# Attention, a dense layer and an expert layer in one kernel: gate logits of three tiles on VectorE, and a first slot filled from twelve tiles

## The chip, the core and the metric

The program runs on one core of one Trainium2 chip. The metric is the device time of one execution in microseconds, as the median of several executions. A profiled execution has a time of its own, and the span of its trace is a little shorter than that time.

## What is computed

Three layers follow one another. All arithmetic is in float32; most matrix products are made as three passes over a high and a low part of each operand, so that they keep float32 accuracy.

```python
# attention: B=4, H=8, S=576, D=64, with rotary positions
attn_out = softmax(rot(q) @ rot(k).T / sqrt(D)) @ v
x = attn_out.transpose(0, 2, 1, 3).reshape(2304, 512)
# dense layer, w_in 512x2048, w_out 2048x512
h = maximum(x @ w_in, 0);  x = (h * h) @ w_out
# expert layer: 8 experts of 512x1024x512, one expert for each token
logits = x @ w_gate + modality_bias[modality_id]
e_idx = argmax(logits, 1);  gate_w = softmax(logits)[arange(N), e_idx]
for e in range(8):
    mask = e_idx == e
    out[mask] = gate_w[mask, None] * (maximum(x[mask] @ w1[e], 0) @ w2[e])
```

## The kernel before, in words

**Blocks and units.** The 2,304 tokens are 18 tiles of 128. The dense layer takes them in five blocks: four of 512 tokens and a fifth of 256 (`BLOCKS`). A block has 16 units, one for each 128 of the 2,048 hidden values; so there are 80 units, and units 64 to 79 are the fifth block. From unit 80 on a unit is one 128-wide chunk of an expert's hidden layer for one slot of tokens.

**One unit.** The loop at line 1092 writes the program in a fixed order. In unit q it writes what hangs in `pre[q]`, then the first half of unit q + 2 (`LA = 2`), then `mid[q]`, then the second half of unit q, then `post[q]`. Each engine works through its own instructions in that order. The first half (`first`, line 680) is: `mm1`, twelve matmuls into `h` (L659); `relu` on ACT (L665), `r` = max(h, 0) scaled; `square` on ACT (L669), which rounds r² into `gh`, the high part; `square_v` on DVE (L673), which puts r² unrounded into `h`; `rest` on DVE (L677), which makes the low part `gl` = h − gh. The second half (`mm2`, L695) adds gh and gl times the output weights into one PSUM bank for each tile.

**Banks.** `h` and all other short-lived PSUM tiles (`junk`, `tp`, `lp`, `rp`, `cp`, `mp`) share a ring of four banks (tag "b", `bufs=4`). In program order the fifth tile takes the bank of the first, and the engine that writes it waits until the last reader of the old one is done.

**Gate logits.** After a block's last unit its output tiles lie in SBUF as `ysb`. For blocks one to three the logits of their tiles are made on DVE by `lg_dve` (L707): one product of a tile with one expert's gate column, summed along the row, 32 for each block, three in a unit; each writes a `junk` bank. The gate columns, copied to all partitions, are the four `wgb` tiles of the tag "wraw". For block four (tiles 12 to 15, in units 64 to 68) and for tiles 16 and 17 they are made on TensorE: `lg_tr` turns a tile with four transposes (L713) and splits it (L716 on ACT, L717 on DVE) into `yt`; `lg_mm` makes eight matmuls into `lp` (L725), from which DVE takes the logits (L727, L728). `choose` then finds each token's expert and `ranks` its rank among the tokens of that expert (L756 to L758).

**Slots.** Experts work on slots of 256 tokens. The first slot (`NE = 2`, so 512 tokens) is filled early, from the most frequent expert among the first `NT0 = 16` tiles: `counts` and `early1` at the end of unit 69 find the expert and each token's position, `early2` (unit 71) turns that into a table with 16 matmuls (L787), `early3` (unit 72) makes indices of it, and four indirect DMAs (`gather`, L942, on POOL's queue) fetch 128 tokens each. `gtrans` (units 74 to 77) turns each gathered tile with four transposes (L952) and splits it in two halves: ACT makes the high part (L965), DVE the low part (L966) of each.

**Expert weights.** `eissue` (L926, on SP's queue) loads a 128-wide chunk of an expert's weights, 512 KB, into a "wraw" tile; `esplit` splits it on ACT (L932) and DVE (L933). The first four are issued from unit 71 on and split at the heads of units 73 to 76, the next four at the heads of units 80 to 83. The first expert half (`emm1`, L979) belongs to unit 80 and is written in unit 78.

**The rest of the table.** After tiles 16 and 17 (units 80 and 81) `final0` to `final4` give every other token a position, and a token of the early expert whose position is below `ET` = 512 stays in the first slot. A last branch (line 1110) runs further slots if more than nine are needed.

Of the kernel before, what the change touches and what calls it, by code (L numbers as in the profile page):

```python
# [9 lines left out]
F32 = mybir.dt.float32  # L10
F32R = mybir.dt.float32r
# [4 lines left out]
ACTF = mybir.ActivationFunctionType  # L16
ALU = mybir.AluOpType
# [434 lines left out]
WF = 2048 + 64  # L452
NE = 2
ET = NE * SLOT
SLOTS = NE + (NTOK - SLOT) // SLOT + E - 1
LAST = NTOK // SLOT - 1
NCOL = 2 * SLOTS
NT0 = 16
BIG = 65536.0
PASSES = ((0, 0), (0, 1), (1, 0))  # L460

# [55 lines left out]
def experts(tc, wts, ps, xT, rD, wexp, mod, wg, mb, cst, ident, yD, out):  # L517
    nc = tc.nc
    with ExitStack() as ctx:
# [10 lines left out]
        def small(shape, dt, name, tag=None):  # L530
            return sb.tile(shape, dt, name=name, tag=tag or name)
# [89 lines left out]
        off = small([128, 1], F32, "off")  # L621
        es0 = small([128, 1], I32, "es0")
        full = small([128, E], I32, "full")
        so, d = small([128, E], F32, "so"), small([128, 1], F32, "d_off")
        es, esi = small([1, SLOTS], F32, "es"), small([1, SLOTS], I32, "esi")
        nh, nhi, tn = small([1, 1], F32, "nh"), small([1, 1], I32, "nhi"), small([1, 1], F32, "tn")
        gv = small([128, NCOL], F32, "gv")
# [42 lines left out]

        def square_v(n):
            h = hs[n]
            nc.vector.scalar_tensor_tensor(out=h, in0=h, scalar=W_SC, in1=rs[n], op0=ALU.mult, op1=ALU.mult)  # L673

        def rest(n):
# [34 lines left out]
        def lg_tr(j):  # L710
            tp = bank([128, DM], "tp")
            for k in range(4):
                nc.tensor.transpose(tp[:, k * 128:(k + 1) * 128], ysb[j][:, k * 128:(k + 1) * 128], ident)  # L713
            t = wts.pool.tile([128, 2, DM], F32R, name="yt", tag="wraw", bufs=NRAW)
            hi, lo = t[:, 0], t[:, 1]
            nc.scalar.activation(out=hi, in_=tp, func=ACTF.Copy)  # L716
            nc.vector.tensor_tensor(out=lo, in0=tp, in1=f32(hi), op=ALU.subtract)  # L717
            yts[j] = hi, lo
# [41 lines left out]
        def counts(j):  # L760
            cp = bank([128, E], "cp")
            nc.tensor.matmul(out=cp, lhsT=one_b, rhs=cum[:, j], start=True, stop=True)
            tables["n"] = cp
# [32 lines left out]
        def early1():  # L796
# [15 lines left out]
            nc.vector.tensor_reduce(out=v_, in_=u, axis=AX.X, op=ALU.add)  # L812
            nc.vector.tensor_scalar(out=v_, in0=v_, scalar1=BIG, scalar2=None, op0=ALU.add)
            rc = split_pos(v_, NT0, "0")
            rhs = small([128, NT0, 2 * NE], F32R, "e_rhs", "et")
            shp = [128, NT0, 2 * NE]
            nc.vector.tensor_tensor(out=rhs, in0=c_io8[:, 0:2 * NE].unsqueeze(1).to_broadcast(shp),
# [12 lines left out]
        def final0():  # L830
            nc.vector.tensor_copy(out=val[:, :, 0], in_=c_id)
            nc.vector.tensor_copy(out=val[:, :, 1], in_=gate)
            nc.vector.tensor_tensor(out=val[:, :, 2], in0=gate, in1=f32(val[:, :, 1]), op=ALU.subtract)
            nc.vector.tensor_scalar(out=so, in0=ohs, scalar1=off, scalar2=None, op0=ALU.mult)
            nc.vector.tensor_scalar(out=d, in0=off, scalar1=-float(ET), scalar2=None, op0=ALU.add)

        def final1():
            cp = tables.pop("n")
# [25 lines left out]
            nc.vector.tensor_copy(out=esi, in_=es)  # L864
            nc.vector.scalar_tensor_tensor(out=add, in0=bc[:, 0], scalar=float(SLOT), in1=so,
                                           op0=ALU.mult, op1=ALU.subtract)
            v_, m_ = small([128, NT], F32, "f_v", "v_"), small([128, NT], F32, "f_m")
            nc.vector.tensor_tensor(out=tmp3, in0=add.unsqueeze(1).to_broadcast([128, NT, E]), in1=rank, op=ALU.add)
            nc.vector.tensor_tensor(out=tmp3, in0=tmp3, in1=oh, op=ALU.mult)
            nc.vector.tensor_reduce(out=v_, in_=tmp3, axis=AX.X, op=ALU.add)  # L870
            nc.vector.tensor_scalar(out=m_, in0=v_, scalar1=float(ET), scalar2=d, op0=ALU.is_lt, op1=ALU.mult)
            nc.vector.tensor_tensor(out=v_, in0=v_, in1=m_, op=ALU.add)
            tables["rc1"] = split_pos(v_, NT, "1")

        def final2():
# [141 lines left out]
        def at(d, n, *fs):  # L1017
            d.setdefault(n, []).extend(fs)

        at(mid, NFC - 1, load_wgb)  # L1020
        for b in range(NB):
# [9 lines left out]
            if b < 3:  # L1031
                jobs = [(j, e) for j in range(j0, j0 + nt) for e in range(E)]
                for q, (j, e) in enumerate(jobs):
                    at(mid, n0 + q // 3, lambda j=j, e=e: lg_dve(j, e))
                at(mid, n0 + 11, lambda j0=j0, nt=nt: choose(j0, j0 + nt))
                at(mid, n0 + 13, lambda j0=j0, nt=nt: ranks(j0, j0 + nt))
            elif b == 3:
                for t in range(4):
                    at(mid, n0 + t, lambda j=j0 + t: lg_tr(j))
                    at(mid, n0 + t + 1, lambda j=j0 + t: lg_mm(j))  # L1040
                at(mid, n0 + 4, lambda j0=j0: choose(j0, j0 + 4))
                at(post, n0 + 5, lambda j0=j0: ranks(j0, j0 + 4), lambda: counts(NT0), early1)
                at(post, n0 + 7, early2)
                at(mid, n0 + 7, lambda: [eissue(m) for m in range(M0, M0 + 3)])
                at(pre, n0 + 8, early3, lambda: [gather(c, True) for c in range(2 * NE)])
                for i in range(4):
                    at(pre, n0 + 9 + i, lambda m=M0 + i: esplit(m, m + 3))
                    at(mid, n0 + 10 + i, lambda t=i: gtrans(NE - 1, t))

        k0 = N - M0  # L1050
        at(mid, N, lambda: lg_tr(16), lambda: lg_tr(17))
# [7 lines left out]
           lambda: esplit(M0 + 10, M0 + 13),  # L1059
           lambda: [gather(2 * NE + 2 + t, False) for t in range(2)], lambda: second(M0 + 7))  # L1060
        for i in range(4):
            at(pre, N + i, lambda m=M0 + 4 + i: esplit(m, m + 3 if m + 3 < M0 + 8 else None))
        for m in range(M0 + 8, M1):
            u = {8: 4, 9: 5, 10: 6, 11: 7}.get(m - M0, m - 4 - M0) + N
            if u != N + 6:
# [169 lines left out]
```

## Time and profile before

| what | us |
|---|---|
| median of 3 runs | 920.58 (919.7 to 921.89) |
| the profiled execution | 921.56 |
| span of its trace | 919.8 |
| PE busy | 895.2 |
| DVE busy | 629.0 |
| ACT busy | 484.3 |

PE is TensorE's matmuls, PEld its weight loads, which run beside the matmuls; DVE is VectorE, ACT ScalarE, POOL GpSimd, SP the queue that issues most DMAs. A matmul's length in the trace contains its way through a pipeline, so lengths of single matmuls overlap; how far the work has moved is read from the starts. Around the span lie 1.76 us of the profiled execution's time. It is 0.98 us above the median.

### The profile page before, as it was taken

How to read it: one execution, taken by the hardware profiler on the slowest of the kernel's cores; microseconds unless marked ns; L12 is line 12 of the kernel's file. 1: busy time of each engine (PE TensorE's matmuls, PEld its weight loads, DVE VectorE, ACT ScalarE, POOL GpSimd, SP SyncE). 2: the span in 40 equal slices, each digit the busy share in tenths (PEclk: the TensorE clock that was granted, in tenths of full speed). 3: DMA queues.
4: the chain of work that ended last, by engine and by line, in shares of the span. 5: the costliest groups of instructions: out<-in, count | busy, mean ns of one | idle time of the engine just before them, and what ended most of it. 6: DMA issues, size and time to landing. Idle time of an engine off the chain costs nothing. (4 is left out here: it accounts for less than half of the span.)

```text
span 919.8 us, 14598 instructions
## 1 busy us (share of the span) xinstructions
PE 895.2 (97%) x5251; PEld 751.5 (82%) x5251; DVE 629.0 (68%) x1197; ACT 484.3 (53%) x956; POOL 287.1 (31%) x229
## 2 busy tenths in 40 slices
PE   7999999999999999999999999999999999999995
PEld 6778778778787887888888888888988899999994
DVE  7998898889888788466545545653655776666650
ACT  6888898868866674322332232224253265555541
POOL 2667687867535555010011001000020322112111
PEclk9999999999999999999999999999999999999998
DMA  5666646546446454410030003001241568767621
GB/s 174 195 167 200 186 150 180 177 110 186 143 146 211 135 183 117 133 35 1 1 116 23 0 1 92 1 1 46 68 140 46 176 205 262 230 220 241 203 93 36
DMA packets 46976, 115.65 MB, mean 126 GB/s; under 512 B 10272, under 2 KB 14384, under 8 KB 46896
## 3 DMA queue, kind: packets, MB, share of 16 engines
q1 hardware_dynamic: 43856, 104.94, 37.1%
q0 software_dynamic: 3040, 9.70, 2.9%
q8 instruction: 43, 0.70, 0.3%
q14 instruction: 37, 0.30, 0.1%
HBM read 92.56 MB, written 15.54 MB: 118 GB/s over the span
## 5 line engine op out<-in xcount | busy, mean ns | idle before, releaser
L665 ACT ACTIVATE r<-h 128x512 f32<-128x512 f32 (+1 forms) x80 | 44.1, 553 | 215.5 <-PE h L659 190.7
L659 PE MATMUL h<-xs,w 128*128 128x512 f32 (+1 forms) x660 | 143.8, 367 | 0.3 <-DVE gl L677 0.3
L673 DVE SCALAR_TENSOR_TENSOR h<-h,r 128x512 f32<-128x512 f32 (+1 forms) x80 | 51.4, 644 | 125.5 <-ACT r L665 125.3
L659 PEld LDWEIGHTS h<-xs,w 128*128 128x128 f32 x660 | 115.8, 188 | 22.0 <-DVE gl L677 0.8
L285 ACT ACTIVATE e<-sc,nmx 128x576 f32<-128x576 f32 x144 | 106.4, 740 | 35.3 <-DVE nmx L274 34.3
L695 PE MATMUL y<-w,gh 128*128 128x512 f32 x396 | 123.2, 392 | 1.2 <-POOL w L514 1.2
L274 DVE TENSOR_REDUCE nmx<-sc 128x1 f32<-128x576 f32 x144 | 106.2, 752 | 23.4 <-PE sc L269 20.1
L269 PE MATMUL sc<-kh,q 128*128 128x288 f32 (+1 forms) x336 | 95.9, 322 | 10.5 <-ACT e L285 9.4
L933 DVE TENSOR_TENSOR w<-eraw,w 128x1024 fp32r<-128x1024 f32 x64 | 78.4, 1225 | 33.9 <-ACT w L932 33.9
L269 PE MATMUL sc<-kl,q 128*128 128x288 f32 (+2 forms) x336 | 88.0, 298 | 0.0
L695 PEld LDWEIGHTS y<-w,gh 128*128 128x128 f32 x396 | 73.3, 188 | 16.4 <-POOL w L514 1.6
L269 PEld LDWEIGHTS sc<-kh,q 128*128 128x128 f32 x336 | 60.7, 189 | 29.0 <-ACT e L285 20.6
L327 PE MATMUL b<-ident,e 128*128 128x128 f32 x640 | 82.5, 275 | 1.1 <-ACT e L285 1.1
L577 POOL TENSOR_TENSOR xraw<-xraw,rbs 128x512 f32<-128x512 f32 (+1 forms) x14 | 16.0, 1148 | 197.5 <-DMA rbs<-rD 194.7
L695 PE MATMUL y<-w,gl 128*128 128x512 f32 x198 | 77.2, 390 | 0.2 <-DVE gl L677 0.2
L979 PEld LDWEIGHTS h<-ye,w 128*128 128x128 f32 x576 | 74.0, 189 | 3.7
L327 PEld LDWEIGHTS b<-ident,e 128*128 128x128 f32 x640 | 74.0, 142 | 1.7 <-ACT e L285 1.3
L979 PE MATMUL h<-ye,w 128*128 128x256 f32 x576 | 74.8, 280 | 0.0
L1002 PE MATMUL y<-w,ge 128*128 128x512 f32 x288 | 74.6, 394 | 0.0
L356 PE MATMUL b<-et,v 128*64 128x288 f32 x512 | 69.5, 412 | 0.0
L932 ACT ACTIVATE w<-eraw 128x1024 fp32r<-128x1024 f32 x64 | 67.4, 1052 | 4.0 <-DMA eraw<-wexp 4.0
L1009 POOL DMA_INDIRECT out<-ob,six x19 | 22.4, 1179 | 137.5 <-ACT ob L1008 105.3
(228 smaller groups left out, 1716.0 us busy)
## 6 DMA issues: line engine op xcount, KB each, us to landing
eraw<-wexp SPq DMA_DIRECT2D x64, 512.0 KB, 4.3
wraw<-wio SPq DMA_DIRECT2D x32, 512.0 KB, 5.2
rawq<-qx SPq DMA_DIRECT2D x15, 576.0 KB, 4.3
rawk<-kx SPq DMA_DIRECT2D x15, 576.0 KB, 4.0
v<-v SPq DMA_DIRECT2D x16, 320.0 KB, 4.8
yD<-ysb SPq DMA_DIRECT2D x18, 256.0 KB, 2.2
xT<-xo SPq DMA_DIRECT2D x12, 288.0 KB, 3.4
xraw<-xT SPq DMA_DIRECT2D x12, 256.0 KB, 2.9
```

The lines of the kernel that those rows point to most:

```text
L269: nc.tensor.matmul(out=o[:, x:x + w], lhsT=q[:, hd, q0:q0 + 128], rhs=k[:, hd, y:y + w], start=(n == 0), stop=(n == len(ops) - 1))
L274: nc.vector.tensor_reduce(out=m, in_=sc(p, j)[:, :, 0:HS], axis=AX.XY, op=ALU.max, negate=True)
L285: nc.scalar.activation(out=e(p)[:, o:o + S].rearrange("p (a b) -> p a b", a=2), in_=sc(p, j)[:, :, 0:HS], func=ACTF.Exp, bias=live[p, f"nm ...
L327: nc.tensor.transpose(t[:, i * 128:(i + 1) * 128], x[:, o:o + 128], ident)
L356: nc.tensor.matmul(out=o[64 * hd:64 * hd + 64], lhsT=lhsT, rhs=rhs, start=(c == 0), stop=(c == 4))
L659: nc.tensor.matmul(out=h, lhsT=w[:, a, k * 128:(k + 1) * 128], rhs=xs[b, k][:, c], start=(k == 0 and i == 0), stop=(k == 3 and i == 2))
L673: nc.vector.scalar_tensor_tensor(out=h, in0=h, scalar=W_SC, in1=rs[n], op0=ALU.mult, op1=ALU.mult)
L695: nc.tensor.matmul(out=yp[t], lhsT=g[a][:, t * 128:(t + 1) * 128], rhs=w[:, c, 512:1024], start=(begin and i == 0), stop=(f == NFC - 1 and ...
L932: nc.scalar.activation(out=w[:, 0], in_=r, func=ACTF.Copy)
L933: nc.vector.tensor_tensor(out=w[:, 1], in0=r, in1=f32(w[:, 0]), op=ALU.subtract)
L979: nc.tensor.matmul(out=h, lhsT=w[:, a, k * 128:(k + 1) * 128], rhs=x[:, c], start=(k == 0 and i == 0), stop=(k == 3 and i == 2))
L1002: nc.tensor.matmul(out=yp[s, t], lhsT=g[a][:, t * 128:(t + 1) * 128], rhs=w[:, c, 512:1024], start=(f == 0 and i == 0), stop=(f == EFC - 1 ...
```

## The change

- **Tiles 12 to 14.** Their logits are made in units 64 to 75 by `lg_dve`, 24 products, two in a unit. Tile 15 stays on TensorE. `choose` and `ranks` for tiles 12 to 15 move to units 78 and 79.
- **Squares.** In the fifth block `square_v` is a second Square on ACT instead of a product on DVE.
- **First slot.** `NT0` is 12. Its table is made at the end of units 61 and 63, and its indices at the head of unit 64; the gathers stay at the head of unit 72. `early1` writes the positions it gives into `pos0` and takes those tokens out of `oh`; `final1` adds `pos0` instead of comparing with `ET`. The formula for `SLOTS` gives 18 instead of 17, so `NCOL` is 36 instead of 34.
- **Buffers.** The `yt` tile moves from the tag "wraw" to "xs". The gate columns stay in "wraw" during the fifth block; a chunk of expert weights is issued (units 67, 70, 73 and 76) as each of their four tiles has had its last product. The first four chunks are split at the heads of units 76, 77, 79 and 80, and each issues the chunk four later.

```diff
--- before.py
+++ after.py
@@ -452,10 +452,10 @@
 WF = 2048 + 64
 NE = 2
 ET = NE * SLOT
-SLOTS = NE + (NTOK - SLOT) // SLOT + E - 1
+NT0 = 12
+SLOTS = NE + (NTOK - NT0 * 128 // E - E) // SLOT + E
 LAST = NTOK // SLOT - 1
 NCOL = 2 * SLOTS
-NT0 = 16
 BIG = 65536.0
 PASSES = ((0, 0), (0, 1), (1, 0))
 
@@ -621,7 +621,7 @@
         off = small([128, 1], F32, "off")
         es0 = small([128, 1], I32, "es0")
         full = small([128, E], I32, "full")
-        so, d = small([128, E], F32, "so"), small([128, 1], F32, "d_off")
+        so, pos0 = small([128, E], F32, "so"), small([128, NT0], F32, "pos0")
         es, esi = small([1, SLOTS], F32, "es"), small([1, SLOTS], I32, "esi")
         nh, nhi, tn = small([1, 1], F32, "nh"), small([1, 1], I32, "nhi"), small([1, 1], F32, "tn")
         gv = small([128, NCOL], F32, "gv")
@@ -670,6 +670,9 @@
 
         def square_v(n):
             h = hs[n]
+            if n >= NFC * (NB - 1):
+                nc.scalar.activation(out=h, in_=rs[n], func=ACTF.Square)
+                return
             nc.vector.scalar_tensor_tensor(out=h, in0=h, scalar=W_SC, in1=rs[n], op0=ALU.mult, op1=ALU.mult)
 
         def rest(n):
@@ -711,7 +714,7 @@
             tp = bank([128, DM], "tp")
             for k in range(4):
                 nc.tensor.transpose(tp[:, k * 128:(k + 1) * 128], ysb[j][:, k * 128:(k + 1) * 128], ident)
-            t = wts.pool.tile([128, 2, DM], F32R, name="yt", tag="wraw", bufs=NRAW)
+            t = sb.tile([128, 2, DM], F32R, name="yt", tag="xs", bufs=5)
             hi, lo = t[:, 0], t[:, 1]
             nc.scalar.activation(out=hi, in_=tp, func=ACTF.Copy)
             nc.vector.tensor_tensor(out=lo, in0=tp, in1=f32(hi), op=ALU.subtract)
@@ -812,6 +815,10 @@
             nc.vector.tensor_reduce(out=v_, in_=u, axis=AX.X, op=ALU.add)
             nc.vector.tensor_scalar(out=v_, in0=v_, scalar1=BIG, scalar2=None, op0=ALU.add)
             rc = split_pos(v_, NT0, "0")
+            nc.vector.scalar_tensor_tensor(out=pos0, in0=v_, scalar=off, in1=v_, op0=ALU.is_lt, op1=ALU.mult)
+            nc.vector.tensor_scalar(out=v_, in0=v_, scalar1=off, scalar2=None, op0=ALU.is_ge)
+            nc.vector.tensor_tensor(out=oh[:, 0:NT0], in0=oh[:, 0:NT0],
+                                    in1=v_.unsqueeze(2).to_broadcast([128, NT0, E]), op=ALU.mult)
             rhs = small([128, NT0, 2 * NE], F32R, "e_rhs", "et")
             shp = [128, NT0, 2 * NE]
             nc.vector.tensor_tensor(out=rhs, in0=c_io8[:, 0:2 * NE].unsqueeze(1).to_broadcast(shp),
@@ -832,7 +839,6 @@
             nc.vector.tensor_copy(out=val[:, :, 1], in_=gate)
             nc.vector.tensor_tensor(out=val[:, :, 2], in0=gate, in1=f32(val[:, :, 1]), op=ALU.subtract)
             nc.vector.tensor_scalar(out=so, in0=ohs, scalar1=off, scalar2=None, op0=ALU.mult)
-            nc.vector.tensor_scalar(out=d, in0=off, scalar1=-float(ET), scalar2=None, op0=ALU.add)
 
         def final1():
             cp = tables.pop("n")
@@ -864,12 +870,11 @@
             nc.vector.tensor_copy(out=esi, in_=es)
             nc.vector.scalar_tensor_tensor(out=add, in0=bc[:, 0], scalar=float(SLOT), in1=so,
                                            op0=ALU.mult, op1=ALU.subtract)
-            v_, m_ = small([128, NT], F32, "f_v", "v_"), small([128, NT], F32, "f_m")
+            v_ = small([128, NT], F32, "f_v", "v_")
             nc.vector.tensor_tensor(out=tmp3, in0=add.unsqueeze(1).to_broadcast([128, NT, E]), in1=rank, op=ALU.add)
             nc.vector.tensor_tensor(out=tmp3, in0=tmp3, in1=oh, op=ALU.mult)
             nc.vector.tensor_reduce(out=v_, in_=tmp3, axis=AX.X, op=ALU.add)
-            nc.vector.tensor_scalar(out=m_, in0=v_, scalar1=float(ET), scalar2=d, op0=ALU.is_lt, op1=ALU.mult)
-            nc.vector.tensor_tensor(out=v_, in0=v_, in1=m_, op=ALU.add)
+            nc.vector.tensor_tensor(out=v_[:, 0:NT0], in0=v_[:, 0:NT0], in1=pos0, op=ALU.add)
             tables["rc1"] = split_pos(v_, NT, "1")
 
         def final2():
@@ -1033,19 +1038,24 @@
                 for q, (j, e) in enumerate(jobs):
                     at(mid, n0 + q // 3, lambda j=j, e=e: lg_dve(j, e))
                 at(mid, n0 + 11, lambda j0=j0, nt=nt: choose(j0, j0 + nt))
-                at(mid, n0 + 13, lambda j0=j0, nt=nt: ranks(j0, j0 + nt))
+                if b < 2:
+                    at(mid, n0 + 13, lambda j0=j0, nt=nt: ranks(j0, j0 + nt))
+                    continue
+                at(post, n0 + 13, lambda j0=j0, nt=nt: ranks(j0, j0 + nt), lambda: counts(NT0), early1)
+                at(post, n0 + 15, early2)
+                at(pre, n0 + 16, early3)
             elif b == 3:
-                for t in range(4):
-                    at(mid, n0 + t, lambda j=j0 + t: lg_tr(j))
-                    at(mid, n0 + t + 1, lambda j=j0 + t: lg_mm(j))
-                at(mid, n0 + 4, lambda j0=j0: choose(j0, j0 + 4))
-                at(post, n0 + 5, lambda j0=j0: ranks(j0, j0 + 4), lambda: counts(NT0), early1)
-                at(post, n0 + 7, early2)
-                at(mid, n0 + 7, lambda: [eissue(m) for m in range(M0, M0 + 3)])
-                at(pre, n0 + 8, early3, lambda: [gather(c, True) for c in range(2 * NE)])
+                at(mid, n0, lambda j=j0 + 3: lg_tr(j))
+                at(mid, n0 + 1, lambda j=j0 + 3: lg_mm(j))
+                for q in range(3 * E):
+                    at(mid, n0 + q // 2, lambda j=j0 + q % 3, e=q // 3: lg_dve(j, e))
+                at(pre, n0 + 8, lambda: [gather(c, True) for c in range(2 * NE)])
                 for i in range(4):
-                    at(pre, n0 + 9 + i, lambda m=M0 + i: esplit(m, m + 3))
+                    at(mid, n0 + (3, 6, 9, 12)[i], lambda m=M0 + i: eissue(m))
+                    at(pre, n0 + (12, 13, 15, 16)[i], lambda m=M0 + i: esplit(m, m + 4))
                     at(mid, n0 + 10 + i, lambda t=i: gtrans(NE - 1, t))
+                at(mid, n0 + 14, lambda j0=j0: choose(j0, j0 + 4))
+                at(mid, n0 + 15, lambda j0=j0: ranks(j0, j0 + 4))
 
         k0 = N - M0
         at(mid, N, lambda: lg_tr(16), lambda: lg_tr(17))
@@ -1059,7 +1069,7 @@
            lambda: esplit(M0 + 10, M0 + 13),
            lambda: [gather(2 * NE + 2 + t, False) for t in range(2)], lambda: second(M0 + 7))
         for i in range(4):
-            at(pre, N + i, lambda m=M0 + 4 + i: esplit(m, m + 3 if m + 3 < M0 + 8 else None))
+            at(pre, N + i, lambda m=M0 + 4 + i: esplit(m))
         for m in range(M0 + 8, M1):
             u = {8: 4, 9: 5, 10: 6, 11: 7}.get(m - M0, m - 4 - M0) + N
             if u != N + 6:
```

## Rows read from the trace of the kernel before

**Rows 1.** Page: granted clock in 40 slices; expert weight issues (KB, us to landing)
```profile
PEclk9999999999999999999999999999999999999998
...
eraw<-wexp SPq DMA_DIRECT2D x64, 512.0 KB, 4.3
```

**Rows 2.** Windows: busy us (count) of PE, PEld, DVE, ACT, POOL; clock; DMA
```profile
628.00:684.00 56.00, 56.00 (x384) 51.37 (x383) 33.21 (x98) 23.51 (x53) 5.17 (x4) 1.00 0.31 104
684.00:737.00 53.00, 52.68 (x255) 43.19 (x255) 31.53 (x89) 15.36 (x24) 7.44 (x7) 1.00 0.29 100
```

**Rows 3.** Waits of PEld from 370 to 905 us: total, times, longest
```profile
PEld h L659 <- DVE gl L677: 0.8, 1, 0.8
PEld mp L787 <- DVE ohr L778: 0.7, 1, 0.7
```

**Rows 4.** Timeline, weight loads, unit with a transposed tile: start, length, engine
```profile
643.58 1.56 PEld L659 LDWEIGHTS h<-xs,we 128*128 128x128 f32 x12
...
645.99 0.42 PEld L713 LDWEIGHTS tp<-ident,ysb 128*128 128x128 f32 x4
...
647.65 1.60 PEld L659 LDWEIGHTS h<-xs,w 128*128 128x128 f32 x12
```

**Rows 5.** Timeline, a fifth-block unit without extra work
```profile
668.46 1.60 PEld L659 LDWEIGHTS h<-xs,w 128*128 128x128 f32 x12
...
669.98 0.30 PEld L695 LDWEIGHTS y<-w,gh 128*128 128x128 f32 x2
...
670.29 0.38 ACT L665 ACTIVATE r<-h 128x256 f32<-128x256 f32 x1 [1.01 <-PE h L659]
...
670.71 0.42 ACT L669 ACTIVATE gh<-r 128x256 fp32r<-128x256 f32 x1
670.71 0.43 DVE L673 SCALAR_TENSOR_TENSOR h<-h,r 128x256 f32<-128x256 f32 x1 [0.17 <-ACT r L665]
...
671.03 1.05 ACT L932 ACTIVATE w<-eraw 128x1024 fp32r<-128x1024 f32 x1
...
671.23 1.59 PEld L659 LDWEIGHTS h<-xs,w 128*128 128x128 f32 x12
```

**Rows 6.** Timeline, weight loads of the first slot's table, and the next unit's
```profile
663.88 1.98 PEld L787 LDWEIGHTS mp<-e_rhs,ohr 128*128 128x128 f32 x16
...
665.78 1.48 PEld L659 LDWEIGHTS h<-xs,w 128*128 128x128 f32 x12
```

**Rows 7.** Timeline, gate products on DVE in the fourth block
```profile
611.32 0.69 DVE L707 SCALAR_TENSOR_TENSOR junk<-ysb,wgb 128x512 f32<-128x512 f32 x1
...
611.92 0.73 DVE L707 SCALAR_TENSOR_TENSOR junk<-ysb,wgb 128x512 f32<-128x512 f32 x1
612.57 0.14 DVE L707 DVE_READ_ACCUMULATOR junk<-ysb,wgb 128x1 f32 x1
```

**Rows 8.** All gate products: duration ns min/median/max, first and last start
```profile
L707 DVE SCALAR_TENSOR_TENSOR junk<-ysb,wgb x96: 687/731/1226, 381.6 to 611.9; 128x512 f32<-128x512 f32 x96
```

**Rows 9.** Timeline, one gathered tile turned and split in two halves
```profile
677.91 0.42 DVE L677 TENSOR_TENSOR gl<-h,gh 128x256 fp32r<-128x256 f32 x1
678.25 0.41 DVE L966 TENSOR_TENSOR yee<-tp,yee 128x256 fp32r<-128x256 f32 x1
678.70 0.39 ACT L965 ACTIVATE yee<-tp 128x256 fp32r<-128x256 f32 x1 [1.33 <-DVE yee L966]
...
679.12 0.42 DVE L966 TENSOR_TENSOR yee<-tp,yee 128x256 fp32r<-128x256 f32 x1 [0.45 <-ACT yee L965]
```

**Rows 10.** Timeline, one tile of expert weights split
```profile
675.12 1.05 ACT L932 ACTIVATE w<-eraw 128x1024 fp32r<-128x1024 f32 x1
...
676.21 1.23 DVE L933 TENSOR_TENSOR w<-eraw,w 128x1024 fp32r<-128x1024 f32 x1 [0.52 <-ACT w L932]
```

**Rows 11.** Timeline, weight loads of the first expert unit
```profile
684.06 0.19 PEld L979 LDWEIGHTS h<-yee,w 128*128 128x128 f32 x1
...
684.68 2.38 PEld L979 LDWEIGHTS h<-yee,w 128*128 128x128 f32 x11 [0.43 <-DVE yee L966]
```

## Prediction, made before the changed kernel was run

> **What bounds the kernel now.** I read the windows of the stretch first, then the waits, then the timeline of single units. In the windows, look at the first two figures: from 628 to 684 us, the fifth block, PE is busy all the time, and from 684 to 737 us for 52.68 of 53 us [rows 2]. DVE has 33.21 and ACT 23.51 us of the 56. The waits say the same: between 370 and 905 us the longest of PE's weight loads are one of 0.8 us for `rest` and one of 0.7 us for the last table's one-hot rows [rows 3]. The clock is at its upper level (2.4 GHz), nine tenths of it or more, in every slice [rows 1]. So PE sets the end here, what leaves PE's program comes off the time, and every new wait of PE goes back on.
>
> The Trainium skill ("Trainium Kernel Development and Optimization", Performance Expectations) says that matmul busy time is a bad metric and weight-load busy share a good one. By it PE is at 51.37 of 56 us, 92% [rows 2], and its other 4.6 us would be room. The short list of waits [rows 3] speaks against it; it is rival four.
>
> **What leaves PE.** A unit with a transposed tile and a tile's logits lasts from weight load 643.58 to 647.65, 4.07 us [rows 4]. A unit with neither lasts from 668.46 to 671.23, 2.77 us [rows 5]. A tile so costs 1.30 us of PE, and three cost 3.90. The first slot's table takes 665.78 − 663.88 = 1.90 us for 16 matmuls [rows 6]; four fewer are 0.48. The last table keeps its 18 matmuls, six columns wider. Its price is bounded by nothing and by the width's share, 6% of the 1.90 us of a table of 16, 0.1 us; I take nothing: even matmuls of four columns took 0.12 us each in the first table [rows 6], so the weight loads set the pace. Together 4.38 us leave.
>
> **What comes to DVE and ACT, and why it doesn't pay in full.** Two products follow each other by 0.60 to 0.65 us [rows 7]; 24 are 15.6 us. DVE had 22.8 us free of the 56 [rows 2] and loses 16 squares of 0.43 us [rows 5], 6.9 us. ACT had 32.5 us free and gains 16 squares. No row shows a Square into PSUM; the nearest is L669, the same shape from the same tile into SBUF, at 0.42 us [rows 5]. I take 0.42, with 0.38 (the relu out of PSUM, same size) and 0.6 as bounds. So both have room in sum. What counts is when a bank of the ring comes free, because the junk tiles turn in it too. I time one unit from its first weight load, using rows 5: relu starts at 1.83, the first square at 2.25, the next ACT instruction at 2.57 (the weight split's place at 671.03). That is now the second square; it ends at 2.99, and DVE starts `rest` 0.04 later, as it does after relu, at 3.03. `rest` takes 0.42 and lets the next DVE instruction start after 0.34 [rows 9], so h is free at 3.45, the products start at 3.37 and 4.02, and the second one's bank is free at 4.02 + 0.65 + 0.14 = 4.81.
>
> - *Units 66 to 73.* In program order each unit takes h, junk, junk. The h of two units later takes the second junk's bank at 2 × 2.77 = 5.54. It is free 0.73 us before. No wait, though each unit hangs on this margin.
> - *Unit 64.* One transposed tile adds a bank, so the next h takes the bank of the h before. PE is there at 2.77 + 0.42 [rows 4] = 3.19, and the bank is free at 3.45. A weight load goes ahead of a waiting matmul (one stood at 684.06 before the pause) [rows 11], which takes some 0.1 us off: 0.15 us; bounds nothing and 0.3.
> - *Unit 74, first gathered tile.* It takes the bank of unit 73's second product, free at 4.81 − 2.77 = 2.04 of unit 74; PE is there when h is through, at 1.52 (669.98 − 668.46) [rows 5]. Wait: 0.5 us.
> - *Unit 75, second gathered tile.* It takes the bank of the first. DVE does `rest` and two products before that tile's low parts, which start at 4.67. The halves go by turns: ACT's second half starts 0.45 after DVE's first, DVE's second 0.42 after that [rows 9]: 5.12 and 5.54, and the bank is free at 5.96. PE passed the first tile at 2.04 + 0.42, began the next h after the second half's 1.25 (671.23 − 669.98) [rows 5] at 3.71 and is there at 5.23. Wait: 0.7 us.
> - *Unit 78, first expert unit.* It waits for the fourth gathered tile's first half: 0.62 us from 684.06 to 684.68, of which the row gives 0.43 as idle [rows 11]. Before it, ACT now has a weight split of 1.05 us [rows 10] at the heads of units 76 and 77, two squares more, and the second tile's half that came late. Carrying the same steps on from 5.96, the fourth tile's first low part ends at about 15.6 where PE is there at 14.0: 1.6 us instead of 0.62, so 0.9 more. Bounds: nothing more, if ACT catches up, and the 1.05 of one whole split on top, 2.0.
>
> These are 2.25 us. The sum: −4.38 + 2.25 = −2.1 us.
>
> At the gathered tiles the trace shows ACT idle for 1.33 us until DVE's half is done, although the halves are different columns [rows 9]. The Trainium skill ("PSUM — Partial Sum Buffer", PSUM bank collisions raise a hardware error) says that accesses of two engines have to be kept apart by bank and not by address; the row agrees. Without that order the second tile would wait some 0.2 us instead of 0.7 and the sum would be −2.6; by the rule and the row it is −2.1.
>
> **What I cost at nothing.** The making of the first table moves to units 61 to 63, with three more small DVE steps and one group of one-hot rows fewer. Those units take 512 columns, so DVE's burst has longer units for cover than before, where it caused none of the long waits [rows 3]; with the cover gone the table's matmuls would wait, as the last table's do, 0.7 us. The eight weight loads only change places. SP has no other transfer between unit 64 and the last two tiles' stores; a load lands in 4.3 us [rows 1], and the tightest, issued in unit 76 and split at the head of unit 80, has four units, over 11 us. It stands behind a load that waits for the first split's low part, one split's 1.23 us [rows 10]; without this cover PE would wait for `esplit`. The gathers keep their place in POOL's queue, and their table is ready eight units earlier. `choose` and `ranks` cost PE three short matmuls in either place; in unit 79 they stand behind the first `gel`, bounds nothing and 0.5 us. In the last table's chain DVE loses two small steps and gets 6% wider products; its wait of 0.7 us [rows 3] stays. `yt` in "xs" frees ACT and DVE in units 80 to 82, where PE did not wait for them: nothing. Routing: the first 12 tiles must hold 512 tokens of their commonest expert, or a tenth slot would run the last branch. With seed 0 I counted 772 of them in the reference's routing, 764 of the next, and both versions come to the same ten slots with the last half not used: no branch.
>
> **Rivals.**
> 1. *No bank waits.* If PE's loads run ahead further than I allow and ACT's square ends earlier, units 64 and 74 to 78 wait as little as before. All 4.4 us come off: 916.2. For it: PE waited for a bank once in the whole stretch [rows 3]. Against: there no unit had two products and a gathered tile.
> 2. *The waits eat the gain.* The second to fourth gathered tiles each wait as the second does (1.4 us more) and the expert unit at its upper bound (1.1 more): waits of 4.7 us, and 920.9, no change. For it: each tile's two halves stand behind products in DVE's queue. Against: units 76 and 77 have no products.
> 3. *Slower: products at the long length.* One product lasted 1.226 us, the median 0.731 [rows 8]. Two of them in every 2.77 us unit: the bank's margin of 0.73 us in units 66 to 73 is gone as soon as a product takes 0.65 + 0.73/2 = 1.0 us; at 1.23 each of eight units waits (2 × 0.58 − 0.73) = 0.4 us, 3.4 in all, and the two gathered tiles wait 1.2 more each. Waits of 8.0 us against 4.4: 924.2. Against: one of 96.
> 4. *PE is not the bound*, the rule on busy time: what PE loses comes back as idle between weight loads. 920.6.
>
> **How the numbers follow.** The sum stands against the profiled execution, 921.56 us (span 919.8 and 1.76 around it), which lies 0.98 above the median of 920.58. Taken off the median: 918.5. The terms' bounds put the forecast between −3.8 (waits of 0.6: nothing in units 64 and 78, half of those in 74 and 75) and −0.4 (0.3, 1.2, 2.0 and 0.5 for unit 79), 916.8 to 920.2. Chances: forecast 0.52, rival one 0.19, two 0.18, three 0.06, four 0.05. I leave out rival three and the far ends: 916.0 to 920.7. About what a measurement of this kernel can tell from no change is 0.2%, 1.84 us, so faster means under 918.74. Of the forecast's own range the part under that is some two thirds, 0.34; with rival one 0.53. The rest of the forecast (0.18), rival four and 0.16 of rival two are the same: 0.39. Slower: 0.08, rival three and the end of rival two.
>
> **What would show it.** Right: no L713 and L725 in units 65 to 68 but for one tile; plain units of 2.77 us with two L707; the table at 12 × 0.12 us; PE idle 0.5 and 0.7 us before the first two groups of L952; the first L979 about 1.5 us late; ACT's square into PSUM near 0.42 us. Wrong: units 66 to 73 longer than 2.77 us (rival three), or PE waiting for L933 or for a load in units 78 to 84, which I cost at nothing.

## The result, and the profile after

| | us | ratio to the kernel before |
|---|---|---|
| before, 11 runs beside it | 921.5 (919.7 to 924.35) | 1 |
| after, 11 runs | 927.83 (925.52 to 931.87) | 1.0067 [1.0048, 1.0086] |
| profiled execution after | 926.26, span 924.4 | |

The change made the kernel slower by 6.3 us where the forecast was 2.1 us faster and its range ended at 920.7.

I looked for the loss in the fifth block first. The waits of PE's weight loads after (columns: who waited <- for whom: total us, times, longest), from 370 to 905 us:

```profile
PEld h L659 <- DVE gl L680: 0.9, 2, 0.6
PEld tp L957 <- PE h L659: 0.7, 1, 0.7
PEld h L984 <- ACT yee L970: 0.6, 1, 0.6
PEld h L984 <- DVE yee L971: 0.4, 1, 0.4
...
PEld tp L957 <- DVE junk L710: 0.4, 1, 0.4
PEld mp L790 <- DVE ohr L781: 0.4, 1, 0.4
```

The six are 3.4 us in all. Before, those of [rows 3] and the 0.43 of [rows 11] were 1.9. They have grown by 1.5 us, less than the 2.25 us that the forecast had put in. The loss lies where nothing was changed. Relu starts of units 18, 62, 88 and 136 (timeline of ACT: start, length, engine, line; the idle time before in brackets), of the kernel before:

```profile
379.54 0.60 ACT L665 ACTIVATE r<-h 128x512 f32<-128x512 f32 x1 [2.12 <-PE h L659]
...
620.13 0.60 ACT L665 ACTIVATE r<-h 128x512 f32<-128x512 f32 x1 [2.15 <-PE h L659]
...
739.61 0.38 ACT L989 ACTIVATE ge<-h 128x256 fp32r<-128x256 f32 x1 [0.32 <-PE h L979]
...
876.38 0.49 ACT L989 ACTIVATE geh<-h 128x384 fp32r<-128x384 f32 x1 [1.17 <-PE h L979]
```

and after:

```profile
377.45 0.60 ACT L665 ACTIVATE r<-h 128x512 f32<-128x512 f32 x1 [2.20 <-PE h L659]
...
624.50 0.60 ACT L665 ACTIVATE r<-h 128x512 f32<-128x512 f32 x1 [2.32 <-PE h L659]
...
742.42 0.39 ACT L994 ACTIVATE ge<-h 128x256 fp32r<-128x256 f32 x1 [0.31 <-PE h L984]
...
880.72 0.49 ACT L994 ACTIVATE geh<-h 128x384 fp32r<-128x384 f32 x1 [1.26 <-PE h L984]
```

The differences between these starts tell where the time went. Units 18 to 62, the dense blocks two to four, have the same instructions in both kernels and take 240.59 us before and 247.05 after, +6.46. Units 62 to 88, where all the changed work is, take 119.48 and 117.92, −1.56. Units 88 to 136, the expert units, take 136.77 and 138.30, +1.53. The first dense units add 0.48 and the end 0.27. Attention was 2.58 us shorter in this execution; the time to the first relu ranged from 284.1 to 289.0 us over all the kernels of this document, most of which change nothing before that point. The sum, 4.6 us, is the difference of the two spans.

What is slow in the dense blocks? Groups of weight loads by form, 390 to 610 us (count, busy us, mean ns of one; then idle us before them). Before:

```profile
L659 PEld LDWEIGHTS h<-xs,w 128*128 128x128 f32 x360 | 67.5, 188 | 14.7 <-DVE gl L677 0.8
L695 PEld LDWEIGHTS y<-w,gh 128*128 128x128 f32 x220 | 41.1, 188 | 8.4
```

After:

```profile
L659 PEld LDWEIGHTS h<-xs,w 128*128 128x128 f32 x348 | 65.3, 188 | 16.4 <-DVE gl L680 0.6
L698 PEld LDWEIGHTS y<-w,gh 128*128 128x128 f32 x216 | 40.4, 188 | 9.6
```

No load got longer (188 ns) and no wait explains it. What grew is the pause from one load to the next: busy and idle without the named wait, over the count, is 81.4/360 = 226 ns before and 81.1/348 = 233 ns after. So every matmul of 512 columns takes 7 ns more, 3%. A dense unit takes 5.61 us in place of 5.44. The granted clock is no part of it: 3% would show in the figure behind the count, which is 1.00, the upper level (2.4 GHz), in both kernels (windows, PE on L659: length, busy us and count, granted clock, DMA share, GB/s). Before:

```profile
480.00:580.00 100.00, 52.90 (x220) 1.00 0.10 30
```

After:

```profile
480.00:580.00 100.00, 53.31 (x216) 1.00 0.10 30
```

What differs is the place of tiles in SBUF, by the addresses of the built programs. The change dropped the 72-byte tile `f_m`. It lies near the top of the pool `m_sb`, which is filled downwards, in steps of 32 bytes. So the large tiles below it moved up by 96 bytes in every partition: `xs` from 189,056 to 189,152, and with it `r`, `gh`, `gl`, `ge`, and `we`, the one dense weight tile in this pool. The other weight tiles, `w` and `wf`, lie in pools filled from below and did not move. Before, all of these, `w` and `wf` too, started 128 bytes past a multiple of 256.

### The profile page after: what moved, and what is told of

It reads as the page before. It is cut to its first block, busy times and chain, and to the rows that moved or that the text cites. A ratio compares the mean times of both kernels' runs of the same rounds, so it can differ in the third digit from the quotient of the medians.

```text
span 924.4 us, 14539 instructions
## 1 busy us (share of the span) xinstructions
PE 902.0 (98%) x5211; PEld 747.1 (81%) x5211; DVE 634.3 (69%) x1220; ACT 487.5 (53%) x969; POOL 285.4 (31%) x229
## 5 line engine op out<-in xcount | busy, mean ns | idle before, releaser
L659 PE MATMUL h<-xs,w 128*128 128x512 f32 (+1 forms) x660 | 147.3, 372 | 0.2 <-DVE gl L680 0.2
L659 PEld LDWEIGHTS h<-xs,w 128*128 128x128 f32 x660 | 116.2, 188 | 25.7 <-DVE gl L680 0.6
L698 PE MATMUL y<-w,gh 128*128 128x512 f32 x396 | 125.2, 397 | 0.0
L676 DVE SCALAR_TENSOR_TENSOR h<-h,r 128x512 f32<-128x512 f32 x64 | 44.6, 698 | 116.1 <-ACT r L665 116.1
L327 PE MATMUL b<-ident,e 128*128 128x128 f32 x640 | 81.4, 273 | 1.1 <-ACT e L285 1.1
L710 DVE SCALAR_TENSOR_TENSOR junk<-ysb,wgb 128x512 f32<-128x512 f32 x120 | 80.3, 721 | 0.0
```

The source lines that it names most:

```text
L327: nc.tensor.transpose(t[:, i * 128:(i + 1) * 128], x[:, o:o + 128], ident)
L659: nc.tensor.matmul(out=h, lhsT=w[:, a, k * 128:(k + 1) * 128], rhs=xs[b, k][:, c], start=(k == 0 and i == 0), stop=(k == 3 and i == 2))
L698: nc.tensor.matmul(out=yp[t], lhsT=g[a][:, t * 128:(t + 1) * 128], rhs=w[:, c, 512:1024], start=(begin and i == 0), stop=(f == NFC - 1 and ...
L710: nc.vector.scalar_tensor_tensor(out=junk, in0=ysb[j], scalar=1.0, in1=wgb[e], op0=ALU.mult, op1=ALU.mult, accum_out=lg[:, j, e:e + 1])
```

## Is it the place? The tiles put back, and the tile alone dropped

**1.** The changed kernel, with `f_v` padded so that the large tiles stand where they stood.

```diff
-            v_ = small([128, NT], F32, "f_v", "v_")
+            v_ = small([128, NT + 24], F32, "f_v", "v_")[:, 0:NT]
```

> The changed kernel, with the one 72-byte tile f_m that it drops given back as room in its neighbour f_v, so that the large tiles of the expert pool (xs, r, gh, gl, ge) stand again where they stood before the change; they had moved up by 96 bytes, from a multiple of 64 to 32 beyond one. Theory A (where they stand sets the pace of the matmuls): units 18 to 62 fall from 5.60 back to 5.44 us, the expert units from 2.81 to 2.77, and the time from 927.8 to 918.5 to 919.5, what the fifth block alone gives. Rival (the pace comes from the change's other parts or from the chip that ran it): units stay at 5.60 and the time at 926 to 930.

Measured: 919.01 us, ratio 0.9959 [0.9943, 0.9976]. Dense units 5.44 us, units 18 to 62 239.97 us, 62 to 88 116.92, 88 to 136 136.77. The instructions are those of the changed kernel, on other addresses. Relu of units 18 and 62:

```profile
379.20 0.60 ACT L665 ACTIVATE r<-h 128x512 f32<-128x512 f32 x1 [2.12 <-PE h L659]
...
619.18 0.60 ACT L665 ACTIVATE r<-h 128x512 f32<-128x512 f32 x1 [2.15 <-PE h L659]
```

**2.** The kernel before without `f_m`, which becomes a part of `tmp3`.

```diff
-            v_, m_ = small([128, NT], F32, "f_v", "v_"), small([128, NT], F32, "f_m")
+            v_, m_ = small([128, NT], F32, "f_v", "v_"), tmp3[:, :, 0]
```

> The kernel before, with nothing changed but that m_ lies in a used-up column of tmp3 instead of the tile f_m of its own; the large tiles move up by 96 bytes as in the changed kernel. Theory A: units of 5.60 us in blocks two to four and 2.81 in the expert layer, 44 x 0.165 + 56 x 0.035 = 9 us more, 930. Rival: no change, 921.5.

Measured: 930.13 us, ratio 1.0092 [1.0065, 1.0119]; units 18 to 62 247.05 us, 88 to 136 138.30, the same to 0.01 us as after the whole change:

```profile
377.99 0.60 ACT L665 ACTIVATE r<-h 128x512 f32<-128x512 f32 x1 [2.20 <-PE h L659]
...
625.04 0.60 ACT L665 ACTIVATE r<-h 128x512 f32<-128x512 f32 x1 [2.32 <-PE h L659]
```

So the place of the tiles is the whole loss, and without it the change gains. Both ways round this is shown, not argued.

## Which places are slow?

Each of these is the kernel before with unused bytes added, by `f_v` larger (all large tiles of `m_sb` lower) or by an unused tile between `xs` and `r`.

```diff
-            v_, m_ = small([128, NT], F32, "f_v", "v_"), small([128, NT], F32, "f_m")
+            v_, m_ = small([128, NT + 8], F32, "f_v", "v_")[:, 0:NT], small([128, NT], F32, "f_m")
```

**3.** All 32 bytes lower (as in the diff). 

> The kernel before, with f_v 32 bytes longer, so that the large tiles move down by 32 bytes. Theory A with a step of 64 bytes: as slow as the kernel without f_m, about 930. If 96 bytes up matter for another reason than the rest by 64 (a collision with one certain tile): no change, 921.5.

**4.** All 64 lower (`NT + 16`). 

> The kernel before, with f_v 64 bytes longer, so that the large tiles move down by 64 bytes, to a multiple of 64 that is not one of 128. Theory A with a step of 64 bytes: no change, 921.5, units of 5.44. With a step of 128: slower, units of 5.5 to 5.6, 926 to 930.

**5.** Only `xs`, `we` and what lies below them 32 lower. 

> The kernel before, with 32 unused bytes between the tiles xs and r: xs (the moving operand of the first dense matmuls) and the small tiles below it go down by 32 bytes, r, gh, gl and ge stay. If a matmul is slowed by the place of either of its operands: the first half's matmuls at 233 ns, the second half's at 226.7, units of 5.52 us, the expert units at 2.77, some 4 us more than before. If only the place of gh and gl counts, through ACT's and DVE's writes: units of 5.44.

**6.** `r`, `gh`, `gl`, `ge` 32 lower, `xs` and `we` 128 lower. 

> The kernel before, with gh, gl, ge and r 32 bytes lower and xs 128 bytes lower (a multiple of 128, as before). If a matmul is slowed by the place of either of its operands: the second half's matmuls, whose weights are gh and gl, at 233 ns and the first half's at 226.7, units of 5.52 us, the second expert matmuls slower as in the changed kernel (213 against 208.5 ns), some 5 us more. If only the moving operand counts: units of 5.44.

**7.** All 128 lower (`NT + 32`). 

> The kernel before, with all large tiles of the expert pool 128 bytes lower. If the pace repeats every 128 bytes: units of 5.44 us and no change. If it repeats every 256 bytes or more, or falls only with the very place of before: another pace.

**8.** All 64 higher (`f_m` in `tmp3`, `NT + 8`). 

> The kernel before without the tile f_m (its values go into a part of tmp3) and with f_v 32 bytes larger, so that the large tiles stand 64 bytes higher. Only shifts of 96 bytes up and of 32, 64 and 128 down were seen so far, all at 5.56 to 5.60 us for a dense unit. Theory one, by the place modulo 256: this is a place not yet seen, and either pace can come. Theory two, the old place alone is the quick one: 5.56 to 5.60 us, time 927 to 931 us.

**9.** All 256 lower (`NT + 64`). 

> The kernel before, with the tile f_v larger and nothing else changed, so that all the large tiles of the expert pool, xs, r, gh, gl and ge, stand 256 bytes lower. Theory one, the pace of the matmuls goes by the place modulo 256 bytes: dense units of blocks two to four stay at 5.44 us, expert units at 2.77, and the time is that of the kernel before within 0.2%, about 921 us. Theory two, what counts is not a repeating part of the address but where these tiles stand to the tiles that do not move (or any other place in this neighbourhood is slow): units of 5.56 to 5.60 us as after every other shift so far, and a time of 928 to 931 us.

| run | us | ratio | units 18 to 62 | dense unit |
|---|---|---|---|---|
| 3: −32 | 931.1 | 1.0089 [1.0058, 1.012] | 246.73 | 5.60 |
| 4: −64 | 929.63 | 1.0069 [1.0048, 1.009] | 245.89 | 5.57 |
| 5: `xs`, `we` −32 | 926.89, one run | | 244.93 | 5.55 |
| 6: −32 and −128 | 928.65, one run | | 246.00 | 5.57 |
| 7: −128 | 931.57, one run | | 246.35 | 5.59 |
| 8: +64 | 928.45, one run | | 245.80 | 5.56 |
| 9: −256 | 920.5 | 0.9999 [0.9984, 1.0014] | 239.95 | 5.44 |

(The dense unit is the median of units 18 to 62.) The clock granted from 380 to 620 us is 1.00 in every one of them, the single runs too. My first theories, steps of 64 and then of 128 bytes, fell with runs 4 and 7. Run 9 fits a period of 256 bytes: that far away all is as before. Run 7 shows that it is no matter of round addresses: there the tiles start at multiples of 256 and are slow.

## The own place, or the place to the other operand?

In the changed kernel, and in most of runs 3 to 8, one group of matmuls is quicker than the others. Weight loads of two successive units of the changed kernel, the second with `we`, which moved together with `xs` (timeline; start, length of the twelve loads):

```profile
469.98 2.75 PEld L659 LDWEIGHTS h<-xs,wf 128*128 128x128 f32 x12
...
475.58 2.71 PEld L659 LDWEIGHTS h<-xs,we 128*128 128x128 f32 x12
```

Before, both took 2.68. That suggests that the place of the two operands to each other counts: the stationary one, which the weight load brings in, and the moving one, which the matmul streams. Two runs part the theories.

**10.** All operands 96 bytes higher: the edit of run 2, and 96 unused bytes below the weights.

```diff
     ident = const.tile([128, 128], F32, name="ident")
+    const.tile([128, 24], F32, name="left")
```

> The kernel before without the tile f_m, so that the large tiles of the expert pool stand 96 bytes higher (as in the run that took 930.13 us), and with 96 unused bytes below the weights, so that the weight tiles w and wf, the raw tiles and the gathered tiles yee stand 96 bytes higher too. All large tiles keep their distances and leave their old place modulo 256 bytes. Theory one, the pace goes by the two operands of a matmul: equal remainders modulo 256 are quick. Dense units take 5.44 us, expert units 2.77, the span from unit 18 to 62 is 240 to 240.6 us, and the time about 921 us within 0.5% (the attention's tiles move as well). Theory two, each large tile must stand at the old remainder by itself: 5.56 us or more, from unit 18 to 62 over 245 us, and 928 us or more.

**11.** That last line alone: only `w`, `wf`, the raw tiles and `yee` are moved. 

> The kernel before with 96 unused bytes below the weights and nothing else: w, wf, the raw tiles and yee stand 96 bytes higher, while xs, r, gh, gl, ge and the dense weight tile we stay. Theory one, equal remainders of the two operands modulo 256 bytes are quick: dense units are slow, 5.56 us or more, because xs with w and gh with w no longer agree; weight loads of xs with we stay at a median of 227 ns, those of xs with w go to 231 to 234. Theory two, what counts is the place of the tiles of the expert pool alone: 5.44 us, as nothing there moved.

Measured: run 10 921.19 us, ratio 1.0 [0.9983, 1.0016]; run 11 931.68 us in one run. Relu of units 18 and 62, first of run 10 (240.60 us apart, 136.97 for the expert units), then of run 11 (247.09):

```profile
381.39 0.60 ACT L665 ACTIVATE r<-h 128x512 f32<-128x512 f32 x1 [2.12 <-PE h L659]
...
621.99 0.60 ACT L665 ACTIVATE r<-h 128x512 f32<-128x512 f32 x1 [2.15 <-PE h L659]
```

```profile
380.80 0.60 ACT L665 ACTIVATE r<-h 128x512 f32<-128x512 f32 x1 [2.21 <-PE h L659]
...
627.89 0.60 ACT L665 ACTIVATE r<-h 128x512 f32<-128x512 f32 x1 [2.31 <-PE h L659]
```

Theory one holds by its main numbers in both runs: tiles of `m_sb` that moved by 96 are quick when the weights moved too, and tiles that did not move are slow when only the weights moved. The mean time from one weight load to the next of the same group, by the pair of operands (from the starts of the loads between 380 and 620 us, pauses over 300 ns left out; `g` is `gh` or `gl`; bold: the pair's remainders modulo 256 differ):

| run | xs, w | xs, we | g, w | g, we |
|---|---|---|---|---|
| before | 226.4 | 226.7 | 226.2 | 226.7 |
| after | **233.3** | 228.2 | **232.7** | 228.8 |
| 5: `xs`, `we` −32 | **232.6** | 229.4 | 228.8 | **233.3** |
| 11: `w`, `wf` +96 | **233.1** | 230.7 | **232.9** | 228.3 |
| 10: all +96 | 226.4 | 226.7 | 226.2 | 226.7 |

In this table every pair whose remainders differ takes 232.6 to 233.3 ns, and every pair whose remainders agree 226 to 231. The other slow runs are less clean: in runs 4 and 6 to 8 pairs that differ go down to 231.1 ns, and the pair of `xs` and `we` in run 6, which agrees, takes 231.1 too. One number of theory one was wrong: this pair was to stay at a median of 227 ns in run 11 and had 231. So a pair that agrees keeps an excess of some 1 to 4 ns when other pairs don't agree.

The starts of the single loads tell where this excess lies. In run 5 the groups of `g` with `w`, which agree, follow groups of `xs` with `w`, which don't. The pauses between the twelve loads of such a group are 225, 231, 236, 229, 232 and 231 ns, and then 227 to its end (means of 29 groups). Groups that differ never settle. The last two pauses of a group have a mean of 226.5 to 228.5 ns for every pair that agrees, in all fifteen kernels, and 230.0 to 234.5 ns for every pair that differs. So a pair that agrees comes to the quick pace within its group, and the excess stands only at its start, behind a slow group. What carries it over is open.

## The parts of the change, with the places kept

**12.** Run 1 with the squares of the fifth block back on DVE.

```diff
-            if n >= NFC * (NB - 1):
-                nc.scalar.activation(out=h, in_=rs[n], func=ACTF.Square)
-                return
```

> The changed kernel with its large tiles put back in their old places, and the second square of the fifth block back on DVE. By the steps of the prediction the low part then starts 0.32 us earlier in a unit (it follows the first square of ACT and not the second), so h and the banks come free earlier. Theory one, the move of the squares to ACT cost and did not help: the units with gathered tiles (74 and 75) take 0.3 to 0.6 us less, units 66 to 73 stay at 2.77 us, and the time is 0 to 1.5 us under that of the changed kernel in the old places, 917.5 to 919. Theory two, DVE has no room for 0.43 us more in the units that have two products, a low part and two halves of a gathered tile (3.0 us of work in 2.77 us): units 74 to 78 together take 0.5 to 2 us more, and the time is 919.5 to 921. The span from the starts of unit 62 to unit 88 was 116.92 us with the squares on ACT.

Measured: 920.72 us, ratio 0.9989 [0.9974, 1.0005], beside another set of runs than run 1's 0.9959. From unit 62 to 88 117.47 us, 0.55 more than run 1. Both theories have a piece: the relus of units 77 and 78 each follow the one before 0.16 and 0.15 us sooner, those of 79 and 80 each 0.56 and 0.57 later. What is lost is lost at the first expert unit (weight loads; idle before, in brackets):

```profile
681.76 0.19 PEld L981 LDWEIGHTS h<-yee,w 128*128 128x128 f32 x1 [0.77 <-ACT yee L967]
683.26 2.35 PEld L981 LDWEIGHTS h<-yee,w 128*128 128x128 f32 x11 [1.31 <-DVE yee L968]
```

In run 1 the same two waits, the last rows here, are 0.68 and 0.44:

```profile
667.92 0.42 PEld L957 LDWEIGHTS tp<-ident,gx 128*128 128x128 f32 x4 [0.40 <-DVE junk L710]
...
671.87 0.42 PEld L957 LDWEIGHTS tp<-ident,gx 128*128 128x128 f32 x4 [0.71 <-PE h L659]
...
680.55 0.19 PEld L984 LDWEIGHTS h<-yee,w 128*128 128x128 f32 x1 [0.68 <-ACT yee L970]
681.18 2.35 PEld L984 LDWEIGHTS h<-yee,w 128*128 128x128 f32 x11 [0.44 <-DVE yee L971]
```

So DVE without the squares is worth 0.55 us in the block. The medians stand 0.3% apart, but their intervals overlap, so this rests on the traces. One execution of each kernel was traced; the three traces of the kernel before at the quick pace (before, runs 9 and 10) lie 0.17 us apart in this stretch.

**13.** Run 1 with the first gathered tiles turned ahead of the gate products in their units.

```diff
+                for i in range(4):
+                    at(mid, n0 + 10 + i, lambda t=i: gtrans(NE - 1, t))
                 for q in range(3 * E):
                     at(mid, n0 + q // 2, lambda j=j0 + q % 3, e=q // 3: lg_dve(j, e))
...
-                    at(mid, n0 + 10 + i, lambda t=i: gtrans(NE - 1, t))
```

> The changed kernel with its large tiles back in place, and in units 74 and 75 the gathered tile's transposes and splits written ahead of that unit's two gate products instead of behind them. Theory of the prediction (the tile waits for a bank behind the products): the waits of 0.4 and 0.7 us before the first two gathered tiles go, about 1 us less than the kernel with the tiles back in place, 918.0. Rival (the wait moves to the next h, whose bank then frees later, or to the first expert unit): no gain, 919.

Measured: 917.94 us, ratio 0.9966 [0.9951, 0.9981]; from unit 62 to 88 115.91 us, 1.01 less than run 1. The waits of 0.40 and 0.71 before L957 are gone, and two of 0.27 and 0.26 before the next `h` stand in their place:

```profile
667.67 1.47 PEld L659 LDWEIGHTS h<-xs,w 128*128 128x128 f32 x12 [0.27 <-DVE gl L680]
...
670.99 1.48 PEld L659 LDWEIGHTS h<-xs,w 128*128 128x128 f32 x12 [0.26 <-DVE gl L680]
```

This version is faster than both kernels: 0.34% under the kernel before. That it beats run 1 (0.41% under) the whole times don't show; the gain of 1.01 us is read from the traces alone.

## Why the prediction was wrong

**The step that failed** is the list "What I cost at nothing". It goes through tables, weight loads, gathers, buffers and routing, but `f_m`, a tile of 72 bytes that the diff drops, is not in it. I read the removed instruction and not the removed allocation. Its price, the changed kernel against run 1, was 7.1 us in dense blocks two to four (247.05 against 239.97), 1.5 in the expert units and 1.0 in the fifth block itself (117.92 against 116.92), more than the 4.4 us that were to leave PE. The prediction's own statement that PE sets the end made it dear: a pace of PE 3% slower has no cover. That alone turned the forecast's sign.

**The steps that were worked out held.** I compare the kernel before with run 1, so at one pace.

- *What leaves PE.* From the relu of unit 62 to that of unit 75: 50.17 before, 45.81 in run 1, −4.36 us. Forecast: −4.38 and a wait of 0.15, together −4.23. Of the changed kernel's timeline, the table of twelve and unit 64:

```profile
641.08 1.53 PEld L790 LDWEIGHTS mp<-e_rhs,ohr 128*128 128x128 f32 x12
642.54 1.47 PEld L659 LDWEIGHTS h<-xs,wf 128*128 128x128 f32 x12
...
645.87 1.47 PEld L659 LDWEIGHTS h<-xs,wf 128*128 128x128 f32 x12 [0.26 <-DVE gl L680]
```

The table takes 1.46 us (forecast 12 × 0.12 = 1.44), and the wait in unit 64 is 0.26 (in run 1 too), where I had 0.15 with a bound of 0.3.

- *One unit with two products.* From one weight load of `h`, after:

```profile
660.65 1.59 PEld L659 LDWEIGHTS h<-xs,w 128*128 128x128 f32 x12
...
662.49 0.39 ACT L665 ACTIVATE r<-h 128x256 f32<-128x256 f32 x1 [1.70 <-PE h L659]
...
662.90 0.42 ACT L669 ACTIVATE gh<-r 128x256 fp32r<-128x256 f32 x1
...
663.23 0.37 ACT L674 ACTIVATE h<-r 128x256 f32<-128x256 f32 x1
...
663.63 0.43 DVE L680 TENSOR_TENSOR gl<-h,gh 128x256 fp32r<-128x256 f32 x1 [1.08 <-ACT h L674]
...
663.97 0.69 DVE L710 SCALAR_TENSOR_TENSOR junk<-ysb,wgb 128x512 f32<-128x512 f32 x1
```

Relu at 1.84, the squares at 2.25 and 2.58, `rest` at 2.98, the first product at 3.32; forecast 1.83, 2.25, 2.57, 3.03 and 3.37. The square into PSUM took 0.37 us, not 0.42: a source in SBUF and a bank as target cost a little less than L669. The products lasted 0.69 to 0.73 us in all 24 cases, so rival three, with 1.23, has no ground, and plain units kept 2.77 us in run 1.

- *Units 74 to 78.* Forecast 0.5, 0.7 and 0.9 more. Run 1 shows 0.40 before the loads of the first tile, 0.71 before the second, and 0.68 + 0.44 at the first expert unit, 0.69 more than the 0.43 of [rows 11]. From the relu of unit 75 to that of unit 88: +1.80 us, forecast 2.1. For the two gathered tiles the cause is the one named, the products ahead of them in DVE's queue: run 13 takes them away and the waits go. The wait at the first expert unit stays in run 13, 0.66 and 0.44 us. That it comes from ACT's weight splits and the tile's late half, as the prediction has it, no run shows.
- *The sum.* Units 62 to 88 in run 1: −2.56 us, forecast −2.1. The whole kernel: −0.41% [−0.57, −0.24], so −2.2 to −5.3 us, which alone would not tell the forecast from rival one; the waits in the trace do.
- *Cost at nothing.* The waits of after hold no weight split and no indices, and the last table waits 0.4 us (0.6 in run 1, 0.7 in [rows 3]).
- *A reading that was off.* The clock stands at nine tenths or more in every slice of [rows 1] but the last, which shows 8. Nothing hangs on it: the stretches above have 1.00.

**Rivals.** One and two fall in run 1: the waits came, and took 2 of the 4.4 us. Four falls there too, since PE's lost work came off the time. The Trainium skill ("Trainium Kernel Development and Optimization", Performance Expectations), which stood behind rival four, would have given no change; run 1 does not agree with it. None of the rivals had a mechanism outside the changed block.

## What to carry to other kernels

When a diff adds, drops or resizes a tile, list what moves with it, even a few bytes, and compare the pace of work that the diff does not touch before the changed part is judged. Where a matmul's two operands come from pools filled from opposite ends, keep their start addresses equal modulo 256 bytes, and pad so that it stays so. This is shown for products whose moving operand has 512 columns. The 256-column tiles of this kernel stand 192 bytes further by design (`OFF` = 48 words of four bytes), so in the fifth block `xs` and `w` agree neither in run 1 nor after the change. They take 127.6 ns from load to load in both (units 66 to 74), though 96 bytes lie between the two places. Whether equal places would serve them no run shows. A wait forecast by adding up one unit's durations, engine by engine, came within some 0.3 us here.

## What the runs showed of the hardware

The pace of back-to-back float32 matmuls of 512 columns at the upper clock level (2.4 GHz) depends on where their two operands start in SBUF, relative to each other and modulo 256 bytes. In the dense units it is 226 ns where all remainders agree, and 231 to 233 ns for every other distance that was tried (the tiles of `m_sb` 32, 64 and 128 lower or 64 and 96 higher, and the weights 96 higher). The weight load itself stays at 188 ns.

The expert units bear this out in part. Their second matmuls (`ge` with `w`, 512 columns), counted as in the table, take 205.8 ns before, 208.4 in run 2, 209.5 in run 3 and 205.9 in run 10, where the places agree again. But in run 4, 64 bytes apart, they take 206.0, and units 88 to 136 last 136.35 us against 136.77 before. So in run 4 the same 64 bytes cost the dense units 2% (5.57 against 5.44 us) and the expert units nothing; why is open. Their first ones, both of whose operands lie in pools that did not move in runs 2 to 4, stayed between 125.9 and 127.5 (126.6 before).

The Trainium skill ("TensorE: Matmul & The Clock Gate", Step-by-step: what each phase is for) says that the weights and the streaming operand come through two read ports of their own, so that a load takes no SBUF bandwidth from a running matmul. By that alone the place of one operand to the other would make no difference; runs 10 and 11 differ by 6.5 us in 44 units, and the measurement decides. Which two accesses meet is not shown by any run here.
